# New costs for the planner, expert blocks of 224 rows, and an earlier load of the second expert's weights

## Chip, cores and metric

One core of a Trainium2 chip. The metric is device time in microseconds (us), the median of three runs. Engines as the profile names them: PE (TensorE) with its weight loads PEld, DVE (VectorE), ACT (ScalarE), POOL (GpSimd), SP (SyncE, which issues most transfers).

## The reference

Three layers in a row, on 1536 tokens of 384 values (2 batches of 768 steps, 8 heads of 48):

```python
# 1. attention: a decaying complex state for each batch and head
a = (a_re + 1j*a_im) * min(|a|, 0.999) / (|a| + 1e-6)
for t in range(768):
    S = a[t][:, None] * S + outer(k[t], v[t])
    y[t] = q[t] @ S.real
# 2. one expert of 8 for each token, capacity 384
e = argmax(x @ w_gate); g = softmax(x @ w_gate)[e]
x = g * (relu(x @ w1[e]) @ w2[e])          # w1: 384 x 1024, w2: 1024 x 384
# 3. dense layer
h = x @ w_in                                # 384 x 2048, given in float64
out = (max(h, 0) + alpha * min(h, 0)) @ w_out
```

The tokens of an expert are taken in order; those beyond its capacity of 384 give zero.

## The kernel before

**Attention.** Twelve tiles of 128 tokens. For each tile, `log_polar`, `turns` and `decay` make logarithms, phases and decays; `decay` forms exp(±sum/8) in `ar` and `ai` on ScalarE and squares each three times (`times`, L384; `DOUBLE` says on which engine, GpSimd for all of them). `edge` (L458 to L471) takes the last decay of a tile from ar. `rotate` multiplies q and k by decays (L542) and by cosine and sine (L547). `attend` transposes them (L572), evicts the transposes kT and qT on ScalarE (L577), forms scores (L591), masks them into pT on VectorE (L597), multiplies by v (L606) and by the state Z (L610), and updates Z (L649, L656). `route` picks the expert of each token and scatters its row to DRAM (`xs_d`, 384 rows for each expert) by GpSimd's indirect transfers.

The order of all this work is not the order of the code. Each operation is entered in a `Plan` with an engine, a cost (`C_ACT`, `C_TT`, `C_SQ`, ...) and a lag until its result can be used; `Plan.order` lists the operations greedily by time and rank, and that list is each engine's order of instructions. The costs act through the order alone; waits are by data. Also in the plan: `clear` zeroes `xs_d` and the unused rows of `ys_d`, and `whole` loads the first expert's weights and splits them.

**Experts.** Every product of the two feed-forward layers is made three times with float32 split into a high part (fp32r) and the rest: weights wh, wl; activations xh, xl and gh, gl. `unit(kk)` loads weight matrix kk in pieces through three staging buffers `st` (L283), rounds the high part on ScalarE (wh, L287) and subtracts on VectorE (wl, L288); matrix 2e is w1 and 2e+1 is w2 of expert e. `ffn` runs an expert's block of `SLOTS` rows in eight steps of 128 hidden units: nine products into hp (L1011) that stream SLOTS columns, gh on ScalarE (L1019) and gl on VectorE (L1020), then for each of two tiles of rows three products into y (L1001) that stream 384 columns. Hooks after each step load and split pieces of the next weights, gather the next expert's rows from `xs_d` (`gather_expert`, L1049) and store results to `ys_d` (L1209). A piece's `wh` stands on ScalarE behind the gh of its step and ahead of the next gh. All these loads wait for the last scatter:

```python
if kk < 2 * NE:
    return unit(kk, pool, eng, scatters[-1:], SYNC)
```

Before the first expert stands `overflow` (L1059): every engine reads the count of the fullest expert and branches past a slow path unless it is over SLOTS. The first expert's rows are put together on chip (`first_expert`). After the branch GpSimd scatters the gates of the first four tiles to `gs_d` (L1111).

**Dense layer.** Three chunks of 512 tokens through the same `ffn` with 16 steps and 512 columns. The first chunk's rows are gathered during the last expert from what the experts before it stored (`first_chunk_rows`, L1151 and L1162); the last expert's own are added on chip (`first_chunk_tail`).

Of the kernel before, what the change touches and what calls it, by code (L numbers as in the profile page):

```python
# [21 lines left out]
P = 128  # L22
# [4 lines left out]
NE = 8  # L27
CAP = 384
SLOTS = 256
# [38 lines left out]
class Plan:  # L68
# [9 lines left out]
    def op(self, engine, cost, fn, use=(), put=(), new=(), after=(), lag=0.06):  # L78
        n = len(self.ops)
        deps = set(after)  # L80
# [16 lines left out]
        self.ops.append(dict(engine=engine, cost=cost, fn=fn, deps=deps, new=list(new), lag=lag, rank=self.rank))  # L97
        return n

    def order(self):  # L100
# [86 lines left out]
def tile_kernel(  # L187
# [150 lines left out]
    def tensor(cost, fn, **kw):  # L338
        return plan.op("T", cost, fn, lag=0.24, **kw)
# [38 lines left out]
    def times(e, n, key):  # L378
        def fn():
            t = tl[key]  # L380
            if e == "A":
                A(out=t, in_=t, func=ACTF.Square)
            else:
                (V if e == "V" else G).tensor_tensor(out=t, in0=t, in1=t, op=ALU.mult)  # L384

        plan.op(e, {"A": C_ACT, "V": C_TT, "G": C_SQ}[e], fn, use=[key], put=[key])

    def log_polar(i):
# [14 lines left out]
        vector(C_TT, lambda: V.tensor_tensor(out=t2(), in0=t2(), in1=tl[f"ai{i}"], op=ALU.mult), use=[t, f"ai{i}"], put=[t])  # L403

        def square():
# [5 lines left out]
        plan.op(SQUARE[i], {"A": C_ACT, "V": C_TT, "G": C_SQ}[SQUARE[i]], square, use=[t], put=[w], new=[("t3", w)])  # L411
# [4 lines left out]
            use=[w, l], put=[l],  # L416
# [6 lines left out]
            use=[w, l], put=[l],  # L423
# [20 lines left out]
    def edge(i):  # L444
# [15 lines left out]
        def spread():  # L460
# [49 lines left out]
    def rotate(i):  # L510
# [13 lines left out]
        else:  # L524
            vector(
                0.4,
# [4 lines left out]
                use=[f"f{i}"], put=[c_],  # L531
# [6 lines left out]
        for dst, e, s, c in (("kk", "ai", "k", ck), ("qq", "ar", "q", cq)):  # L538
# [10 lines left out]
            vector(C_STT, scaled, use=[ek, sk], put=[ek])  # L549
            vector(C_WIDE, turned, use=[ek, c_], put=[dk], new=[(dst, dk)])  # L550

    def attend(i):
# [12 lines left out]
        def tr(hh):  # L565
            for src, nm, sc in ((kk, "kT", 1.0 / LAM), (qq, "qT", 1.0)):
# [16 lines left out]
                plan.op(e, {"A": 0.6, "V": 0.68}[e], evict, use=[p], put=[t])  # L583

        def scores(hh):
# [14 lines left out]
            vector(0.7, mask, use=[p], put=[t])  # L600
# [43 lines left out]
        scalar(0.5, out, use=[f"y{i}"], put=[f"x{i}"], new=[("x", f"x{i}")])  # L644
        if not last:
            zv = Z[:, 0:DM].rearrange("p (h d) -> p h d", d=D)
            vector(
                0.56,
# [6 lines left out]
                0.6,  # L655
# [3 lines left out]
                use=[zk, f"ez{i}"], put=[zk],  # L659
# [4 lines left out]
    def route(g):  # L664
# [11 lines left out]
        for j, i in enumerate(tl_):  # L676
# [18 lines left out]
            scalar(0.5, evict, use=[p], put=[x])  # L695
# [60 lines left out]
        vector(1.1 + 0.3 * n, choose, use=[f"lg{g}", "racc", "ready"], put=["racc", f"oc{g}"])  # L756
        tensor(0.3, count, use=[f"oc{g}", "ready"], put=[f"pp{g}"], new=[("y" if tail else "u", f"pp{g}")])
        vector(1.3, place, use=[f"pp{g}"], put=[f"si{g}"])
        for i in tl_:
# [14 lines left out]
            pool(1.2, scatter, use=[f"si{g}", f"x{i}", "zeroed"], put=[f"xs{i}"], lag=2.0)  # L774
# [5 lines left out]
    def gather_early():  # L780
        for j in range(SLOTS // P):
            rows0.append(raw.tile([P, DM], F32, tag="ar", name="rows0", bufs=RAW["ar"]))
            ins = G.dma_start(out=rows0[j], in_=xs_d[j * P:(j + 1) * P, :])
# [7 lines left out]
    def first_expert():  # L791
# [9 lines left out]
        for c in range(KC):  # L801
            for j in range(SLOTS // P):
                ins = add(c, rows0[j], ident, slice(j * P, (j + 1) * P))
# [43 lines left out]
    def clear():  # L847
# [17 lines left out]
    def whole(kk):  # L865
# [5 lines left out]
        for j in range(c // m):  # L871
# [16 lines left out]
            scalar(0.95, high, use=[key], put=[f"h{key}"])  # L888
            vector(1.05, low, use=[key, f"h{key}"], put=[f"l{key}"])
# [90 lines left out]
    def split_rows(rows, xh, xl, j, behind=None):  # L980
        pt = pm.tile([P, KC, P], F32, tag="tr", name="pt")
        for c in range(KC):
            follow(T.transpose(pt[:, c, :], rows[:, c * P:(c + 1) * P], ident), behind, "h")  # L983
        sl = slice(j * P, (j + 1) * P)
# [3 lines left out]
    def ffn(xh, xl, N, units, sink, hooks, tail=None):  # L988
        nt = N // P
        ys = [pm.tile([P, DM], F32, tag="y", name="y", bufs=4) for _ in range(nt)]  # L990
# [47 lines left out]
        for t in range(nt):  # L1038
            o = fp.tile([P, DM], F32, tag="o", name="o", bufs=3)
# [3 lines left out]
    def gather_expert(e):  # L1043
# [3 lines left out]
        for j in range(SLOTS // P):  # L1047
            rows.append(fp.tile([P, DM], F32, tag="rows", name="rows", bufs=4))
            ins = nc.sync.dma_start(out=rows[j], in_=xs_d[e * CAP + j * P:e * CAP + (j + 1) * P, :])  # L1049
# [3 lines left out]
    def split_expert(xh, xl, rows, behind):  # L1053
        for j in range(SLOTS // P):
            split_rows(rows[j], xh, xl, j, behind)
        return xh, xl

    def overflow():
        fullest = nc.values_load(most[0:1, 0:1], min_val=0, max_val=NT)  # L1059
        with tc.If(fullest > SLOTS):  # L1060
            for e in range(NE):
                r0 = e * CAP + SLOTS
                rows = fp.tile([P, DM], F32, tag="rows", name="rows", bufs=4)
                after_scatters(nc.sync.dma_start(out=rows, in_=xs_d[r0:r0 + P, :]))
# [206 lines left out]
```

## Time and profile before

| | us |
|---|---|
| median of 3 runs | 592.74 (592.65 to 595.22) |
| profiled execution | 592.36 |
| its span, first to last instruction | 590.6 |
| TensorE busy | 527.0 (89%) |
| VectorE busy | 356.2 (60%) |
| ScalarE busy | 308.5 (52%) |
| GpSimd busy | 110.7 (19%) |
| granted TensorE clock, mean | 0.949 |

Matmuls overlap, so TensorE's busy time counts a product longer than the step from one to the next; the time of a stream of products is read from the chain of waits. A group of instructions is one line of the kernel with its operation and tiles.

### The profile page before, as it was taken

The numbers are of one execution on the slowest core, as the hardware profiler recorded it, in microseconds if no ns is written. First come the engines' busy times: TensorE is split into PE (matmuls) and PEld (weight loads), VectorE is DVE, ScalarE is ACT, GpSimd is POOL, SyncE is SP. The second block draws the span as 40 slices with busy tenths as digits, with TensorE's granted clock in tenths as the row PEclk, the third lists the DMA queues.
The fourth block names the chain that finished last, engine by engine and source line by source line (L and its number), as shares of the span: only waits on it lengthen the run. The fifth ranks groups of instructions, "written<-read, shape, count | busy, mean of one in ns | idle before, by whom it ended". The sixth has DMA issues, their size and how long they took to land.

```text
span 590.6 us, 8614 instructions
## 1 busy us (share of the span) xinstructions
PE 527.0 (89%) x3270; PEld 483.3 (82%) x3270; DVE 356.2 (60%) x617; ACT 308.5 (52%) x565; POOL 110.7 (19%) x119
## 2 busy tenths in 40 slices
PE   1677969796898968799999999899999999999996
PEld 0466869795888868799999998688899999989986
DVE  2558798869638431677765796979783333333322
ACT  6577866675334231666655643446464443453433
POOL 2518084708027221000000003030200000000000
PEclk9967998899798798899999999999999999999999
DMA  8994334201000108888768746435400000010001
GB/s 281 354 344 147 95 94 139 89 14 42 0 28 1 55 29 136 275 260 257 253 205 322 234 148 222 161 130 156 149 20 35 22 0 1 0 54 2 0 2 53
DMA packets 37407, 71.01 MB, mean 120 GB/s; under 512 B 4105, under 2 KB 30098, under 8 KB 36594
## 3 DMA queue, kind: packets, MB, share of 16 engines
q1 hardware_dynamic: 35570, 65.30, 34.3%
q0 software_dynamic: 1792, 5.12, 2.5%
q8 instruction: 27, 0.44, 0.3%
q14 instruction: 18, 0.15, 0.1%
HBM read 55.84 MB, written 14.56 MB: 119 GB/s over the span
## 4 chain that ended last, share of the span: by engine, by line
PE 75%; DVE 9%; DMA 6%; POOL 3%; ACT 3%; issue 2%; SPq 0%; POOLq 0%; ACTq 0%; DVEq 0%
PE hp L1011 26%; PE y L1001 26%; PE sc L591 5%; PE y L606 4%; PE y L610 3%; DMA st<-in_moe_w 2%; PE pt L484 2%; POOL ai L384 2%; PE pkT L572 2%; DVE Z L656 2%; PE u L623 1%; POOL ar L384 1%; PE pt L487 1%; DMA gs_d<-gate,sidx 1%; PE pt L983 1%
## 5 line engine op out<-in xcount | busy, mean ns | idle before, releaser
L1011 PE MATMUL hp<-xh,wh 128*128 128x256 f32 (+1 forms) x336 | 112.5, 335 | 3.1 <-PEq L1060 2.9
L1001 PE MATMUL y<-wh,gh 128*128 128x384 f32 x320 | 109.7, 343 | 4.9 <-ACT gh L1019 4.9
L1011 PE MATMUL hp<-xl,wh 128*128 128x256 f32 (+1 forms) x336 | 111.9, 333 | 0.6 <-DVE xl L1188 0.6
L1011 PE MATMUL hp<-xh,wl 128*128 128x256 f32 (+1 forms) x336 | 111.9, 333 | 0.0
L1001 PE MATMUL y<-wl,gh 128*128 128x384 f32 x320 | 107.9, 337 | 0.0
L1001 PE MATMUL y<-wh,gl 128*128 128x384 f32 x320 | 89.3, 340 | 0.2 <-DVE gl L1020 0.2
L288 DVE TENSOR_TENSOR wl<-st,wh 128x768 fp32r<-128x768 f32 (+1 forms) x63 | 67.4, 1070 | 31.3 <-ACT wh L287 30.7
L287 ACT ACTIVATE wh<-st 128x768 fp32r<-128x768 f32 (+1 forms) x63 | 58.9, 935 | 30.6 <-DMA st<-in_moe_w 18.1
L1026 DVE SCALAR_TENSOR_TENSOR gn<-gn,nalp,gp 128x512 f32<-128x512 f32 x48 | 35.9, 748 | 62.7 <-ACT gp L1025 62.7
L1011 PEld LDWEIGHTS hp<-xh,wh 128*128 128x128 f32 x336 | 64.5, 192 | 8.6 <-issue 3.0
L1011 PEld LDWEIGHTS hp<-xl,wh 128*128 128x128 f32 x336 | 64.6, 192 | 5.7 <-DVE xl L1188 1.0
L1011 PEld LDWEIGHTS hp<-xh,wl 128*128 128x128 f32 x336 | 64.6, 192 | 5.0
L1001 PEld LDWEIGHTS y<-wh,gh 128*128 128x128 f32 x320 | 60.6, 189 | 7.4 <-ACT gh L1019 5.6
L1024 ACT ACTIVATE gn<-hp 128x512 f32<-128x512 f32 x48 | 28.7, 597 | 71.5 <-PE hp L1011 60.5
L1001 PEld LDWEIGHTS y<-wl,gh 128*128 128x128 f32 x320 | 60.5, 189 | 1.2
L1001 PEld LDWEIGHTS y<-wh,gl 128*128 128x128 f32 x320 | 56.9, 189 | 1.2 <-DVE gl L1020 0.7
L1028 DVE TENSOR_TENSOR gl<-gn,gh 128x512 fp32r<-128x512 f32 x48 | 33.1, 690 | 29.5 <-ACT gh L1027 29.4
L384 POOL TENSOR_TENSOR ar<-ar 128x384 f32<-128x384 f32 x36 | 35.2, 977 | 77.1 <-ACT ar L438 77.0
L1019 ACT ACTIVATE gh<-hp 128x256 fp32r<-128x256 f32 x64 | 24.2, 380 | 45.3 <-PE hp L1011 45.3
L606 PE MATMUL y<-vt,pT 128*128 128x128 f32 x192 | 38.8, 297 | 7.0 <-DVE pT L597 7.0
L1027 ACT ACTIVATE gh<-gn 128x512 fp32r<-128x512 f32 x48 | 30.2, 630 | 22.3 <-DVE gn L1026 21.1
L384 POOL TENSOR_TENSOR ai<-ai 128x384 f32<-128x384 f32 x36 | 40.1, 1114 | 0.0
(166 smaller groups left out, 869.3 us busy)
## 6 DMA issues: line engine op xcount, KB each, us to landing
st<-in_moe_w SPq DMA_DIRECT2D x24, 512.0 KB, 4.6
st<-in_moe_w SPq DMA_DIRECT2D x32, 384.0 KB, 3.6
sw<-in_moe_w_in SPq DMA_DIRECT2D x6, 1024.0 KB, 6.2
sw<-in_moe_w_out SPq DMA_DIRECT2D x8, 768.0 KB, 4.3
xs_d<-zero SPq DMA_DIRECT2D x1, 4608.0 KB, 15.4
ys_d<-o SPq DMA_DIRECT2D x16, 192.0 KB, 2.7
rows<-xs_d SPq DMA_DIRECT2D x14, 192.0 KB, 4.6
ar<-in_a_re SPq DMA_DIRECT2D x12, 192.0 KB, 3.8
```

Of the source, the lines that this page charges most:

```text
L287: follow(A(out=wh[:, js], in_=st, func=ACTF.Copy), behind, "A")
L288: ins = eng[j].tensor_tensor(out=wl[:, js], in0=st, in1=wh[:, js].bitcast(F32), op=ALU.subtract)
L384: (V if e == "V" else G).tensor_tensor(out=t, in0=t, in1=t, op=ALU.mult)
L591: T.matmul(out=sc[:, h, :], lhsT=tl[f"kT{i}{hh}"][:, h, :], rhs=tl[f"qT{i}{hh}"][:, h, :], start=True, stop=True)
L606: T.matmul(out=y()[:, o:o + P], lhsT=tl[f"pT{i}{hh}"][:, h, :], rhs=tl[vk][:, o:o + P], start=True, stop=(c == 0))
L1001: T.matmul(out=ys[t], lhsT=a[:, sl], rhs=b[:, f, :], start=(ft == 0 and m == 0), stop=(ft == nf - 1 and m == 2))
L1011: ins = T.matmul(out=hp, lhsT=a[:, c, fs], rhs=b[:, c, :], start=(n == 0), stop=(n == 3 * KC - 1))
L1019: last["A"] = A(out=gh, in_=hp, func=ACTF.Relu)
L1024: A(out=gn, in_=hp, func=ACTF.Relu, scale=-1.0)
L1026: V.scalar_tensor_tensor(out=gn, in0=gn, scalar=nalp[:, ft:ft + 1], in1=gp, op0=ALU.mult, op1=ALU.add)
L1027: last["A"] = A(out=gh, in_=gn, func=ACTF.Copy)
L1028: last["V"] = V.tensor_tensor(out=gl, in0=gn, in1=gh.bitcast(F32), op=ALU.subtract)
```

## The change

- `DOUBLE`: the three squarings of ar go to ScalarE, those of ai stay on GpSimd.
- All planner costs and lags are replaced by the durations from a trace. Operations get a mark `port`; marked ones of VectorE and GpSimd exclude each other in the plan. Marked are the squarings on GpSimd and VectorE's operations on two SBUF operands.
- `SLOTS` is 224 instead of 256, in two tiles of `TW` = 112 rows instead of 128. The overflow branch is taken above 224; its blocks are twice 80 rows. `clear` zeroes 160 instead of 128 rows of each expert in `ys_d`.
- The loads of weight matrix 2 (w1 of the second expert) no longer wait for the last scatter.

```diff
-SLOTS = 256
+SLOTS = 224
+ST = 2
+TW = SLOTS // ST
+OW = (CAP - SLOTS) // 2
...
-DOUBLE = (('GGG', 'GGG'),) * NTL
+DOUBLE = (('AAA', 'GGG'),) * NTL
...
-C_ACT, C_BIAS, C_TT, C_STT, C_PS, C_WIDE, C_SQ = 0.52, 0.61, 0.6, 0.62, 0.56, 1.0, 1.0
+C_ACT, C_BIAS, C_TT, C_STT, C_PS, C_WIDE, C_SQ = 0.415, 0.51, 0.47, 0.5, 0.47, 0.87, 0.79
+LAG = {'A': 0.14, 'V': 0.13, 'G': 0.1, 'T': 0.28, 'S': 2.2}
...
-    def op(self, engine, cost, fn, use=(), put=(), new=(), after=(), lag=0.06):
+    def op(self, engine, cost, fn, use=(), put=(), new=(), after=(), lag=None, port=False):
         n = len(self.ops)
+        lag = LAG[engine] if lag is None else lag
...
-                t = max([free.get(o["engine"], 0.0)] + [done[d] for d in o["deps"]])
+                t = max([free.get(o["engine"], 0.0), free.get("port", 0.0) if o["port"] else 0.0] + [done[d] for d in o["deps"]])
...
             free[o["engine"]] = t + o["cost"]
+            if o["port"]:
+                free["port"] = t + o["cost"]
...
-        plan.op(e, {"A": C_ACT, "V": C_TT, "G": C_SQ}[e], fn, use=[key], put=[key])
+        plan.op(e, {"A": C_ACT, "V": C_TT, "G": C_SQ}[e], fn, use=[key], put=[key], port=e != "A")
...
-            vector(C_STT, scaled, use=[ek, sk], put=[ek])
-            vector(C_WIDE, turned, use=[ek, c_], put=[dk], new=[(dst, dk)])
+            vector(0.53, scaled, use=[ek, sk], put=[ek], port=True)
+            vector(C_WIDE, turned, use=[ek, c_], put=[dk], new=[(dst, dk)], port=True)
...
         for e in range(NE):
-            nc.sync.dma_start(out=ys_d[e * CAP + SLOTS:(e + 1) * CAP, :], in_=zero)
-        for r in range((NE - 1) * CAP, (NE - 1) * CAP + SLOTS, P):
-            nc.sync.dma_start(out=ys_d[r:r + P, :], in_=zero)
+            nc.sync.dma_start(
+                out=ys_d[e * CAP + SLOTS:(e + 1) * CAP, :].rearrange("(r p) d -> p r d", p=OW),
+                in_=zero[0:OW].unsqueeze(1).to_broadcast([OW, 2, DM]),
+            )
+        for t in range(ST):
+            r = (NE - 1) * CAP + t * TW
+            nc.sync.dma_start(out=ys_d[r:r + TW, :], in_=zero[0:TW])
...
         if kk < 2 * NE:
-            return unit(kk, pool, eng, scatters[-1:], SYNC)
+            return unit(kk, pool, eng, scatters[-1:] if kk > 2 else (), SYNC)
...
-        for j in range(SLOTS // P):
-            rows.append(fp.tile([P, DM], F32, tag="rows", name="rows", bufs=4))
-            ins = nc.sync.dma_start(out=rows[j], in_=xs_d[e * CAP + j * P:e * CAP + (j + 1) * P, :])
+        for j in range(ST):
+            rows.append(fp.tile([TW, DM], F32, tag="rows", name="rows", bufs=4))
+            ins = nc.sync.dma_start(out=rows[j], in_=xs_d[e * CAP + j * TW:e * CAP + (j + 1) * TW, :])
...
         with tc.If(fullest > SLOTS):
-            for e in range(NE):
-                r0 = e * CAP + SLOTS
+            for e, r0 in ((e, e * CAP + SLOTS + i * OW) for e in range(NE) for i in range(2)):
...
-        ffn(*xe, SLOTS, [e], store, hooks, first_chunk_tail if e == NE - 1 else None)
+        ffn(*xe, SLOTS, TW, [e], store, hooks, first_chunk_tail if e == NE - 1 else None)
```

The rest of the diff gives new numbers and `port` marks to the other planned operations and writes tiles of TW rows where tiles of 128 stood.

## Rows read from the trace of the kernel before

**Rows 1.** Stretches: busy us (count) of PE, PEld, DVE, ACT, POOL; PEclk, DMA share, GB/s.
```profile
11.00:219.00 208.00, 171.35 (x1192) 150.85 (x1192) 141.12 (x297) 119.26 (x225) 87.36 (x87) 0.88 0.31 106
219.00:382.00 163.00, 152.72 (x1047) 148.55 (x1047) 111.52 (x169) 85.97 (x157) 10.45 (x9) 0.98 0.71 224
382.00:590.60 208.60, 202.71 (x1031) 183.65 (x1031) 100.69 (x144) 96.13 (x173) 10.76 (x8) 0.99 0.14 46
```
**Rows 2.** Waits of PE, 10 to 218 us: in total, times, longest.
```profile
PE pz L458 <- POOL ar L384: 9.0, 4, 4.6
PE y L606 <- DVE pT L597: 7.0, 3, 5.3
PE sc L591 <- ACT qT L577: 4.3, 5, 2.0
```
**Rows 3.** Stretches at the lower clock; columns as in rows 1.
```profile
114.00:120.40 6.40, 6.40 (x32) 6.33 (x33) 4.35 (x8) 3.23 (x6) 1.05 (x1) 0.50 0.10 32
149.00:155.30 6.30, 6.27 (x31) 5.80 (x31) 1.79 (x5) 1.53 (x3) 0.00 (x0) 0.56 0.00 0
186.00:194.60 8.60, 7.33 (x43) 6.55 (x42) 6.90 (x20) 2.75 (x5) 1.91 (x2) 0.66 0.01 3
...
239.90:243.30 3.40, 3.40 (x16) 3.40 (x15) 2.81 (x5) 2.40 (x5) 0.00 (x0) 0.50 0.84 275
```
**Rows 4.** One line's instructions: ns min/median/max, first and last start.
```profile
L656 DVE TENSOR_TENSOR Z<-Z,ezs x10: 548/576/7156, 47.5 to 204.5; 96x384 f32<-96x384 f32 x10
```
**Rows 5.** Timeline of POOL (start, us): first and last of nine squarings.
```profile
140.41 0.85 POOL L384 TENSOR_TENSOR ai<-ai 128x384 f32<-128x384 f32 x1
...
146.68 0.81 POOL L384 TENSOR_TENSOR ai<-ai 128x384 f32<-128x384 f32 x1
```
**Rows 6.** Chain that ended last (start, us, what), one piece each.
```profile
66.21 0.89 PE sc L591 x8
...
266.20 1.07 PE hp L1011 x9
...
465.99 2.08 PE hp L1011 x9
```
**Rows 7.** Timeline of PE in the first expert, with its idle time before.
```profile
231.04 0.44 PE L1001 MATMUL y<-wh,gh 128*128 128x384 f32 x1 [0.90 <-ACT gh L1019]
...
238.88 0.45 PE L1001 MATMUL y<-wh,gh 128*128 128x384 f32 x1 [3.03 <-ACT gh L1019]
```
**Rows 8.** Timeline of ACT in the same time.
```profile
235.89 1.06 ACT L287 ACTIVATE wh<-st 128x1024 fp32r<-128x1024 f32 x1 [4.63 <-DMA st<-in_moe_w]
```
**Rows 9.** Groups by line of POOL: busy us, mean ns, idle before.
```profile
L384 POOL TENSOR_TENSOR ai<-ai 128x384 f32<-128x384 f32 x36 | 40.1, 1114 | 0.0
L384 POOL TENSOR_TENSOR ar<-ar 128x384 f32<-128x384 f32 x36 | 35.2, 977 | 77.1 <-ACT ar L438 77.0
```
**Rows 10.** Timeline of ACT, two activations back to back.
```profile
43.43 0.93 ACT L401 ACTIVATE l<-ar 128x384 f32<-128x384 f32 x2
```
**Rows 11.** Timeline of DVE in the last expert.
```profile
368.27 0.42 DVE L1162 TENSOR_SCALAR rows<-rows,gate 128x384 f32<-128x384 f32 x1 [3.49 <-DMA rows<-ys_d,eidx]
```
**Rows 12.** The seventh expert's stretch; columns as in rows 1.
```profile
340.00:357.00 17.00, 17.00 (x126) 16.97 (x126) 16.93 (x24) 8.13 (x18) 0.00 (x0) 1.00 0.45 152
```
**Rows 13.** Transfers: count, KB each, median us from issue to landing.
```profile
xs_d<-zero SPq DMA_DIRECT2D x1, 4608.0 KB, 15.4
...
gs_d<-gate,sidx POOLq DMA_INDIRECT x4, 8.8
```
**Rows 14.** Waits of SP's queue: in total, times, longest.
```profile
SPq L283 <- DMA xs_d<-x,sidx: 2.2, 1, 2.2
```
**Rows 15.** Timeline of SP's queue (start, us of issue).
```profile
221.84 0.35 SPq L283 DMA_DIRECT2D st<-in_moe_w  x1
222.66 1.17 SPq L1049 DMA_DIRECT2D rows<-xs_d  x2
223.89 0.89 SPq L283 DMA_DIRECT2D st<-in_moe_w  x2
```

More of the change, by code (lines that the diff above doesn't have):

```diff
@@ L96, in op @@
         deps.discard(n)
-        self.ops.append(dict(engine=engine, cost=cost, fn=fn, deps=deps, new=list(new), lag=lag, rank=self.rank))
+        self.ops.append(dict(engine=engine, cost=cost, fn=fn, deps=deps, new=list(new), lag=lag, rank=self.rank, port=port))
         return n
@@ L409, in square @@
                 (V if SQUARE[i] == "V" else G).tensor_tensor(out=t3(), in0=t2(), in1=t2(), op=ALU.mult)
-        plan.op(SQUARE[i], {"A": C_ACT, "V": C_TT, "G": C_SQ}[SQUARE[i]], square, use=[t], put=[w], new=[("t3", w)])
+        plan.op(SQUARE[i], {"A": C_ACT, "V": C_TT, "G": C_SQ}[SQUARE[i]], square, use=[t], put=[w], new=[("t3", w)],
+                port=SQUARE[i] != "A")
         scalar(C_ACT, lambda: A(out=t3(), in_=t3(), func=ACTF.Ln, bias=1.0), True, use=[w], put=[w])
@@ L415, in log_polar @@
             lambda: V.scalar_tensor_tensor(out=t1(), in0=t3(), scalar=0.5, in1=t1(), op0=ALU.mult, op1=ALU.add),
-            use=[w, l], put=[l],
+            use=[w, l], put=[l], port=True,
         )
@@ L422, in log_polar @@
             lambda: V.scalar_tensor_tensor(out=t1(), in0=t1(), scalar=LN999, in1=t3(), op0=ALU.min, op1=ALU.subtract),
-            use=[w, l], put=[l],
+            use=[w, l], put=[l], port=True,
         )
@@ L530, in rotate @@
                 ),
-                use=[f"f{i}"], put=[c_],
+                use=[f"f{i}"], put=[c_], port=True,
             )
@@ L642, in out @@
             A(out=xt[i], in_=y()[:, 0:DM], func=ACTF.Copy)
-        scalar(0.5, out, use=[f"y{i}"], put=[f"x{i}"], new=[("x", f"x{i}")])
+        scalar(0.39, out, use=[f"y{i}"], put=[f"x{i}"], new=[("x", f"x{i}")])
         if not last:
@@ L658, in attend @@
                 ),
-                use=[zk, f"ez{i}"], put=[zk],
+                use=[zk, f"ez{i}"], put=[zk], port=True,
             )
@@ L772, in scatter @@
                 scatters.append(ins)
-            pool(1.2, scatter, use=[f"si{g}", f"x{i}", "zeroed"], put=[f"xs{i}"], lag=2.0)
+            pool(1.2, scatter, use=[f"si{g}", f"x{i}", "zeroed"], put=[f"xs{i}"], lag=2.0, port=False)
     early = []
@@ L978, in need, with split_rows, ffn @@
                 piece(None)
-    def split_rows(rows, xh, xl, j, behind=None):
-        pt = pm.tile([P, KC, P], F32, tag="tr", name="pt")
+    def split_rows(rows, xh, xl, j, w=P, behind=None):
+        pt = pm.tile([P, KC, w], F32, tag="tr", name="pt")
         for c in range(KC):
-            follow(T.transpose(pt[:, c, :], rows[:, c * P:(c + 1) * P], ident), behind, "h")
-        sl = slice(j * P, (j + 1) * P)
+            follow(T.transpose(pt[:, c, :], rows[0:w, c * P:(c + 1) * P], ident[0:w, 0:w]), behind, "h")
+        sl = slice(j * w, (j + 1) * w)
         A(out=xh[:, :, sl], in_=pt, func=ACTF.Copy)
         V.tensor_tensor(out=xl[:, :, sl], in0=pt, in1=xh[:, :, sl].bitcast(F32), op=ALU.subtract)
-    def ffn(xh, xl, N, units, sink, hooks, tail=None):
-        nt = N // P
-        ys = [pm.tile([P, DM], F32, tag="y", name="y", bufs=4) for _ in range(nt)]
+    def ffn(xh, xl, N, w, units, sink, hooks, tail=None):
+        nt = N // w
+        ys = [pm.tile([w, DM], F32, tag="y", name="y", bufs=4) for _ in range(nt)]
         nf = FT * len(units)
@@ L1053, in split_expert @@
     def split_expert(xh, xl, rows, behind):
-        for j in range(SLOTS // P):
-            split_rows(rows[j], xh, xl, j, behind)
+        for j in range(ST):
+            split_rows(rows[j], xh, xl, j, TW, behind)
         return xh, xl
@@ L1060, in overflow @@
         with tc.If(fullest > SLOTS):
-            for e in range(NE):
-                r0 = e * CAP + SLOTS
-                rows = fp.tile([P, DM], F32, tag="rows", name="rows", bufs=4)
-                after_scatters(nc.sync.dma_start(out=rows, in_=xs_d[r0:r0 + P, :]))
+            for e, r0 in ((e, e * CAP + SLOTS + i * OW) for e in range(NE) for i in range(2)):
+                rows = fp.tile([OW, DM], F32, tag="rows", name="rows", bufs=4)
+                after_scatters(nc.sync.dma_start(out=rows, in_=xs_d[r0:r0 + OW, :]))
                 a1 = []
@@ L1136, in first_chunk @@
             V.tensor_scalar(out=oh, in0=io, scalar1=srel[:, j:j + 1], scalar2=None, op0=ALU.is_equal)
-            for t in range(SLOTS // P):
-                T.transpose(ot[:, t, j * P:(j + 1) * P], oh[:, t * P:(t + 1) * P], identb)
+            for t in range(ST):
+                T.transpose(ot[:, t, j * P:(j + 1) * P], oh[:, t * TW:(t + 1) * TW], identb)
         os = []
-        for t in range(SLOTS // P):
-            o = fp.tile([P, n * P], F32R, tag="gn", name="os")
+        for t in range(ST):
+            o = fp.tile([TW, n * P], F32R, tag="gn", name="os")
             A(out=o, in_=ot[:, t], func=ACTF.Copy)
@@ L1172, in first_chunk_tail @@
         xh, xl, gsl, os, pts = (chunk0[k] for k in ("xh", "xl", "gsl", "os", "pts"))
-        for t in range(SLOTS // P):
-            h = fp.tile([P, DM], F32R, tag="gh", name="yh", bufs=3)
-            l = fp.tile([P, DM], F32R, tag="gl", name="yl", bufs=3)
+        for t in range(ST):
+            h = fp.tile([TW, DM], F32R, tag="gh", name="yh", bufs=3)
+            l = fp.tile([TW, DM], F32R, tag="gl", name="yl", bufs=3)
             A(out=h, in_=ys[t], func=ACTF.Copy, scale=gsl[:, t:t + 1])
```

69 lines of the change are left out of this document (35 added, 34 removed).

## The prediction

> **What bounds the kernel now.** I read the page first, then the stretch view by stage, because the share of busy time is an average over three stages with different limits [rows 1]. From 11 to 219 us (attention, routing, scatters) no engine is full: TensorE is busy 171 of 208 us at a granted clock of 0.88, VectorE 141, ScalarE 119, GpSimd 87. From 219 to 382 us (eight experts) TensorE is busy 152.7 of 163. From 382 us on (the dense layer) it is busy 202.7 of 208.6 at 0.99; nothing of the change is in that stage. So a gain must come from waits in the first stage and from TensorE work or waits in the second.
>
> The view of TensorE's waits in the first stage says what it stood for [rows 2]: 9.0 us for GpSimd's squarings of ar, 7.0 us for the masked scores pT of VectorE, 5.3 of that in one piece, and 4.3 us for ScalarE's evictions qT. Three stretches at the lower of the two clock levels (1.2 instead of 2.4 GHz) follow such gaps [rows 3].
>
> The 5.3 us piece has a visible cause. The line that multiplies Z takes 0.55 to 0.58 us, but once 7.16 us [rows 4], and in just that time GpSimd runs nine squarings back to back, from 140.41 to 147.5 us [rows 5]. VectorE, with two operands in SBUF, stood still until GpSimd's row ended.
>
> In the second stage the chain of waits is one product after another: nine first-layer products of 256 columns in 1.07 us [rows 6]. The exception is its start: TensorE waits 0.9 and 3.0 us for gh [rows 7], because ScalarE is in order and gh stands behind wh, which waits for the second expert's weights [rows 8].
>
> **Part 1, squarings and planner.** 36 squarings of ar leave GpSimd: 35.2 of its 75.3 us of squarings [rows 9]. They go to ScalarE: two activations of this size take 0.93 us, 0.465 each [rows 10], so 36 take 16.7 us. ScalarE is busy 119 of 208 us, so there is room on average; behind each squaring stand evictions like qT that TensorE waits for already. The longer half of the chain ar, ai on one engine also becomes two shorter ones: a tile's six squarings at 0.98 to 1.11 us take some 6.3 us now, then three on GpSimd, 2.3 to 3.3 us, beside three on ScalarE, 1.4.
>
> What can go at most: 9.0 us for ar and 5.3 us for the blocked Z, 14.3 together; and of the three slow-clock stretches of the stage 6.4 x 0.50 + 6.3 x 0.44 + 8.6 x 0.34 = 8.9 us. That is 23.2 us. What is late next: the other squarings, ai, which keep GpSimd and the contention (a group of two tiles still makes a row of six, 4.7 us at 0.78 each), and ScalarE. The new costs, lags and the rule that marked VectorE and GpSimd operations exclude each other only reorder each engine's queue; they cost nothing themselves, and the trace can't price an order that it hasn't seen. Bounds: nothing gained, since a new order can lose what it gains, and four fifths of 23.2, 18.6 us. I take two fifths, **-9.3 us**, since ScalarE's evictions, already the third of the waits, get 16.7 us of work in front of them.
>
> On this block the Trainium skill (SBUF — State Buffer, Who interferes with whom) says that the one of VectorE and GpSimd that starts first holds the shared port pair for its whole instruction. Read strictly, Z would have waited for one squaring; the row says nine. By the page alone the length of a GpSimd row wouldn't matter, and this term would fall by two fifths of 5.3, to -7.2 us; the measurement decides.
>
> **Part 2, blocks of 224.** The first layer streams 224 columns instead of 256. Nine products of 512 columns take 2.08 us, of 256 1.07 us [rows 6]: (2.08 - 1.07) / (9 x 256) = 0.438 ns per column, so 14.0 ns per product. 8 experts x 8 blocks x 9 products = 576, so 8.1 us. The second layer has 112 instead of 128 stationary columns but still streams 384: counted as nothing, since the chain shows products set by what they stream. The last expert can't use its 1.0 us: it waits for the rows gathered from the seventh's stores, until 368.27 us [rows 11], and that chain of transfers doesn't shorten. So **-7.1 us**. Bounds: -8.1; and -5 if the experts from 340 to 357 us gain nothing either, where VectorE is busy 16.93 of 17.00 us with weight conversions [rows 12]. Evictions, gathers and stores of 224 rows shrink by an eighth beside TensorE's work: nothing.
>
> Clearing ys_d writes 160 instead of 128 rows for each expert and 224 instead of 256 for the last: 0.34 MB more. At the 4608 KB in 15.4 us of xs_d's clearing that is 1.1 us of transfer [rows 13], with the loads of k, q, ar and ai behind it in SP's queue. No wait of TensorE for them shows after 11 us: 0, at worst +1.1.
>
> The gate of the overflow branch becomes 224. The reference's default inputs give the fullest expert 220 rows, so it stays untaken.
>
> The Trainium skill (TensorE: Matmul & The Clock Gate, Back-to-back issue gap) gives for streams of weight loads and products 81 ns at 128 columns and 131 ns at 512. As an estimate from that page 32 columns are 4.2 ns, 2.4 us in all, and the sum below would be 4.7 us higher. The trace has 229 ns at 512 and disagrees.
>
> **Part 3, the second expert's first weights.** Three loads of 512 KB (w1 of expert 1) no longer wait for the last scatter. They can't pass the branch on the fullest expert, so they start when SP leaves it: it waited 2.2 us for the scatter and issued at 221.84, the other two at 223.89, behind two gathers of rows [rows 14, 15]. Now the first goes at 219.6 and, if the gathers don't stand between, the others 0.4 us apart, before the four scatters of gates, which take 8.8 us to land and share the transfer engines [rows 13]. Before, the second wh could start only at 235.89 [rows 8]. To be won: the 3.9 us of waiting for gh, and the slow stretch at 239.9, 3.4 x 0.5 = 1.7 [rows 3]: 5.6 us. What is late next: the gathered rows, now behind 1.5 MB, and the fourth weight load, which needs a freed st buffer. Bounds 0 (the gathers keep their place in front, so only the first load moves) and 5.6; I take **-3.5 us**, nearer to the upper end because 2.2 us of head start at the front of the queue matter most while the gates' scatters haven't begun.
>
> **Sum.** -9.3 - 7.1 - 3.5 = -19.9. The profiled execution took 592.36 us (span 590.6), the median of the three runs is 592.74, so nearly the same: 592.4 - 19.9 = **572.5 us**.
>
> **Rivals.** *ScalarE takes GpSimd's place.* TensorE's waits for ScalarE grow by what those for GpSimd shrink, and part 1 gives 0: 592.4 - 10.6 = 581.8. For it: 16.7 us more on an in-order engine that feeds the scores. Against: ScalarE idles 89 of 208 us. Chance 0.22.
>
> *The early load gains nothing*, because the gathers stay in front or the gates' scatters slow it as before: 576. For it: the second load's 12 us from its issue to wh. Against: the 2.2 us wait is real. Chance 0.08.
>
> *The narrower product is slower* (the other side). No row has an fp32r product under 256 columns. If such a one ran like a plain f32 product, two records of 0.89 / 8 = 0.111 us for 128 columns each [rows 6], that is 1.74 ns per column, a product of 224 would take 0.390 instead of 0.119 us: 576 x 0.271 = +156, and 592.4 - 12.8 + 156 = 736 us. It decides against the change from 12.8 / 576 = 22 ns above the 0.119 us of now. Against: from 512 to 256 columns the time halves without a knee. Chance 0.07. The overflow branch being taken has 0.01.
>
> The forecast has the rest, 0.62, and its own range is 562 to 580. Range: it takes in both rivals on this side, 561 (four fifths of the waits, all of part 3) to 586 (nothing of part 1, 5 and about 1.5 us of the others). Below 0.5% (3 us) nothing can be told from no change. Faster 0.86 (forecast and first two rivals but for a tail of 0.06), same 0.05, slower 0.09 (the last two, and 0.01 of a bad order).
>
> **What would show it.** In the profile after: 36 activations more on ScalarE's squaring line and 36 squarings on GpSimd; no Z multiply of 7 us, and TensorE's wait for ar under 4 us; the last scatter before 212 instead of 219 us; nine products in 0.95 us; the three weight loads issued by 221 us (less the shift of the first stage) and TensorE's wait for gh under 2 us; the dense stage again 208 us. The prediction fails if nine products take over 1.07 us, if the end of the scatters doesn't move, or if TensorE's waits for ScalarE in the first stage double.

## The result

The changed kernel takes 561.07 us (median of four executions, 560.52 to 564.88) against 593.49 (592.65 to 595.22) of before: a ratio of 0.946, 95% interval 0.942 to 0.951. The forecast was 572.5 with 561 to 586: the time lies at the very edge of the range, and the sum behind it came out so only because two errors partly cancel. The profiled execution took 561.13 us, span 559.0.

The stretch view of after, cut at the first product of the first expert and the first 512-column product of the dense layer (columns as in [rows 1]):

```profile
0.00:186.90 186.90, 157.31 (x1193) 138.50 (x1193) 124.89 (x306) 139.06 (x273) 54.62 (x69) 0.95 0.42 137
186.90:348.70 161.80, 148.83 (x1046) 144.10 (x1046) 105.44 (x166) 83.57 (x155) 6.87 (x7) 0.96 0.75 215
348.70:559.00 210.30, 203.79 (x1032) 183.49 (x1032) 101.47 (x146) 96.62 (x174) 11.23 (x8) 0.99 0.15 49
```

The same cuts through before stand at 221.7 and 381.4 us:

```profile
0.00:221.70 221.70, 171.63 (x1193) 151.16 (x1193) 144.72 (x306) 126.86 (x237) 91.54 (x105) 0.88 0.34 114
221.70:381.40 159.70, 152.22 (x1047) 148.34 (x1047) 110.23 (x167) 84.92 (x155) 8.45 (x7) 0.98 0.72 225
381.40:590.60 209.20, 203.19 (x1032) 183.81 (x1032) 101.29 (x145) 96.73 (x174) 10.76 (x8) 0.99 0.14 47
```

So the first stage became 34.8 us shorter (forecast 9.3), the experts 2.1 us longer (forecast 10.6 shorter: 7.1 and 3.5), the dense layer 1.1 us longer (forecast 0).

In the first stage TensorE does the same 1193 products in 157.3 instead of 171.6 us, at a granted clock of 0.95 instead of 0.88, and idles 29.6 instead of 50.1 us. Its waits in after, 10 to 184 us (in total, times, longest):

```profile
PE pl L445 <- DVE l L431: 10.1, 1, 10.1
PE pz L467 <- ACT ar L389: 5.6, 2, 4.0
PE pz L467 <- DMA k<-in_k: 4.4, 1, 4.4
PE y L615 <- DVE pT L606: 2.2, 4, 0.7
PE sc L600 <- ACT qT L586: 0.9, 1, 0.9
```

The first row is the start-up. Not only the wait for ar is smaller [rows 2]: pT fell from 7.0 to 2.2 us, qT from 4.3 to 0.9. The Z multiply that once took 7.16 us [rows 4] takes at most 1.16 us (one line's instructions, ns min/median/max):

```profile
L665 DVE TENSOR_TENSOR Z<-Z,ezs x10: 542/548/1161, 41.8 to 168.7; 96x384 f32<-96x384 f32 x10
```

In the experts nine products of 224 columns take 0.99 to 1.00 us in the chain of waits, where 256 took 1.07 [rows 6]:

```profile
226.60 0.99 PE hp L1024 x9
...
236.43 1.00 PE hp L1024 x9
```

And the second expert's weights come no sooner. The timeline of SP's queue:

```profile
187.43 0.69 SPq L290 DMA_DIRECT2D st<-in_moe_w  x1
190.98 0.48 SPq L1062 DMA_DIRECT2D rows<-xs_d  x2
191.51 0.90 SPq L290 DMA_DIRECT2D st<-in_moe_w  x2
```

GpSimd's timeline, the last scatter of rows and the first of four of gates:

```profile
183.87 1.01 POOL L770 DMA_INDIRECT xs_d<-x,sidx  x1 [0.30 <-issue]
185.18 0.97 POOL L1123 DMA_INDIRECT gs_d<-gate,sidx  x1 [0.30 <-issue]
```

ScalarE's timeline, the first two pieces of w1 of the second expert:

```profile
195.52 1.06 ACT L294 ACTIVATE wh<-st 128x1024 fp32r<-128x1024 f32 x1 [6.02 <-DMA gs_d<-gate,sidx]
203.68 1.06 ACT L294 ACTIVATE wh<-st 128x1024 fp32r<-128x1024 f32 x1 [6.86 <-DMA st<-in_moe_w]
```

The order is that of before [rows 15]: one load, two gathers, two loads. The second load needs 12.2 us from its issue at 191.51 to wh at 203.68; before it was 12.0 (223.89 to 235.89, [rows 8, 15]). TensorE waits for gh 2.9 and 4.6 us instead of 0.9 and 3.0 [rows 7] (its waits, 184 to 220 us: in total, times, longest):

```profile
PE y L1014 <- ACT gh L1032: 7.5, 2, 4.6
```

The first expert takes 31.5 us instead of 27.3, the second 22.2 instead of 20.4, so the two lose 6.0 us. The first expert's stretch, in after and in before, columns as in [rows 1]:

```profile
186.90:218.36 31.46, 22.78 (x127) 21.49 (x127) 11.14 (x17) 10.99 (x20) 2.48 (x3) 0.77 0.86 177
```

```profile
221.70:248.95 27.25, 22.35 (x131) 21.21 (x132) 11.84 (x18) 11.29 (x20) 2.90 (x3) 0.87 0.82 201
```

It also runs at a lower granted clock, 0.77 instead of 0.87: in the 2 us ahead of it the clock is 0.50 in after and 1.00 in before.

### The profile page after: what moved, and what is told of

Same layout as the page of the kernel before. It is cut to its first block, busy times and chain, and to the rows that moved or that the text cites. A ratio compares the mean times of both kernels' runs of the same rounds, so it can differ in the third digit from the quotient of the medians.

```text
span 559.0 us, 8603 instructions
## 1 busy us (share of the span) xinstructions
PE 509.9 (91%) x3270; PEld 466.1 (83%) x3270; DVE 331.8 (59%) x617; ACT 319.3 (57%) x601; POOL 72.7 (13%) x83
## 4 chain that ended last, share of the span: by engine, by line
PE 45%; DMA 10%; issue 5%; DVE 3%; ACT 2%; POOL 1%; SPq 0%; POOLq 0%; ACTq 0%
PE y L1014 23%; PE hp L1024 22%; DMA st<-in_moe_w 5%; DMA rows<-ys_d,gidx 2%; DMA ys_d<-o 1%; DVE wl L295 1%; DMA rows<-ys_d,eidx 1%; ACT wh L294 1%; PE pt L996 1%; DVE st L283 0%; POOL rows L1110 0%; ACT o L1053 0%; DMA out<-o 0%; POOL rows L1163 0%; DVE gl L1033 0%
## 5 line engine op out<-in xcount | busy, mean ns | idle before, releaser
L1014 PE MATMUL y<-wh,gh 128*128 128x384 f32 (+1 forms) x320 | 109.2, 341 | 7.6 <-ACT gh L1032 7.5
L1024 PE MATMUL hp<-xh,wh 128*128 128x224 f32 (+1 forms) x336 | 111.1, 331 | 3.3 <-DVEq L1073 2.1
L1024 PE MATMUL hp<-xl,wh 128*128 128x224 f32 (+1 forms) x336 | 110.8, 330 | 1.8 <-DVE xl L999 1.0
L1024 PE MATMUL hp<-xh,wl 128*128 128x224 f32 (+1 forms) x336 | 110.7, 329 | 0.0
L1014 PE MATMUL y<-wl,gh 128*128 128x384 f32 (+1 forms) x320 | 108.1, 338 | 0.0
L1014 PE MATMUL y<-wh,gl 128*128 128x384 f32 (+1 forms) x320 | 89.5, 341 | 1.3 <-DVE gl L1033 1.0
L1014 PEld LDWEIGHTS y<-wh,gh 128*128 128x128 f32 (+1 forms) x320 | 58.7, 183 | 10.0 <-ACT gh L1032 7.9
L1014 PEld LDWEIGHTS y<-wl,gh 128*128 128x128 f32 (+1 forms) x320 | 58.7, 183 | 1.5
L1014 PEld LDWEIGHTS y<-wh,gl 128*128 128x128 f32 (+1 forms) x320 | 55.2, 184 | 3.2 <-DVE gl L1033 2.2
L615 PEld LDWEIGHTS y<-vt,pT 128*128 128x128 f32 x192 | 29.3, 198 | 3.5 <-DVE pT L606 3.0
```

Of the source, the lines that this page charges most:

```text
L615: T.matmul(out=y()[:, o:o + P], lhsT=tl[f"pT{i}{hh}"][:, h, :], rhs=tl[vk][:, o:o + P], start=True, stop=(c == 0))
L1014: T.matmul(out=ys[t], lhsT=a[:, sl], rhs=b[:, f, :], start=(ft == 0 and m == 0), stop=(ft == nf - 1 and m == 2))
L1024: ins = T.matmul(out=hp, lhsT=a[:, c, fs], rhs=b[:, c, :], start=(n == 0), stop=(n == 3 * KC - 1))
```

## The experiments

Twelve kernels ran. Stage times are those of each one's profile: first stage (to the first expert's first product), experts, dense layer. Ratios are to the kernel before, run beside it.

| kernel | median us | ratio, 95% interval | first stage | experts | dense |
|---|---|---|---|---|---|
| before | 593.49 | | 221.7 | 159.7 | 209.2 |
| after | 561.07 | 0.946 (0.942 to 0.951) | 186.9 | 161.8 | 210.3 |
| e1, squarings alone | 582.88 | 0.985 (0.982 to 0.989) | 211.2 | 159.2 | 209.2 |
| e2, costs and lags alone | 585.83 | 0.991 (0.987 to 0.994) | 214.4 | 160.0 | 209.0 |
| e3, costs, lags, port marks | 582.13 | 0.980 (0.972 to 0.988) | 207.9 | 166.2 | 210.5 |
| e4, costs, lags, squarings | 565.01 | 0.957 (0.951 to 0.962) | 191.8 | 158.7 | 209.2 |
| e12, lags and squarings | 572.40 | 0.966 (0.960 to 0.972) | 202.2 | 159.0 | 209.2 |
| e5, after with 256 rows | 561.90 | 0.948 (0.942 to 0.954) | 186.2 | 164.7 | 209.5 |
| e6, after with the wait back | 556.48 | 0.936 (0.932 to 0.941) | 187.6 | 159.4 | 209.9 |
| e7, gates moved in the code | 560.53 | 0.944 (0.939 to 0.948) | 186.6 | 161.6 | 209.9 |
| e8, loads ahead of gathers | 560.23 | 0.943 (0.936 to 0.951) | 184.8 | 159.9 | 212.0 |
| e9, gates held back | 559.92 | 0.946 (0.942 to 0.951) | 186.4 | 161.7 | 209.3 |
| e10, loads before the branch | 552.53 | 0.935 (0.930 to 0.940) | 186.6 | 152.7 | 210.2 |
| e11, e9 and e10 | 554.37 | 0.937 (0.933 to 0.941) | 188.0 | 154.0 | 210.2 |

Each stage time is of one execution. After and e5 to e11 have the same plan for the first stage, and its time in their eight profiles goes from 184.8 to 188.0 us, so a difference of two or three microseconds between two such times shows nothing.

### The first stage: e1 to e4 and e12

**e1**, before with one edit:

```diff
-DOUBLE = (('GGG', 'GGG'),) * NTL
+DOUBLE = (('AAA', 'GGG'),) * NTL
```

> Before with one edit: the three squarings of ar of each group go to ScalarE (DOUBLE 'AAA','GGG'), with the old costs, the old lags and no port marks. The first stage (to the first product of the first expert) took 221.7 us before and 186.9 after, 34.8 less. Theory A (the squarings on GpSimd and what they block on VectorE held the stage): at least 22 of the 34.8 come back, first expert's product by 200 us, whole time 572 or less. Theory B (the order made from the new costs and lags did it): under 12 us, first product after 210, time 581 or more. Theory C (the port marks did it): likewise under 12 us; B and C part in the next runs.

Measured: 211.2, that is 10.5 us less. Theory A falls, as B and C wanted: the squarings alone bring a third of the 34.8, about what the forecast had for the whole part. GpSimd's squarings already stand in rows of three here, and no VectorE instruction of the stage takes over 1.27 us: the blocked Z multiply is gone, and 24.3 us of the gain are still to come from elsewhere.

**e2**, before with the new `C_...` costs and `LAG`, but `DOUBLE` old and no port in `Plan.order`.

> Before with the new costs and lags of the planner alone; all squarings stay on GpSimd and no operation excludes another. Theory A: the 36 GpSimd squarings of ar still stand in front of TensorE, gain under 8 us, first product after 213, time 585 to 593. Theory B: at least 18 us, first product by 204, time 575 or less. Theory C: under 8 us, as A.

Measured: 7.3 us less, so theory B falls as well, as put. The longest VectorE instruction, in its timeline:

```profile
133.95 7.09 DVE L428 SCALAR_TENSOR_TENSOR l<-l,w 128x384 f32<-128x384 f32 x1 [1.24 <-ACT w L425]
```

GpSimd's timeline, the first and the last of eight:

```profile
134.31 0.86 POOL L388 TENSOR_TENSOR ar<-ar 128x384 f32<-128x384 f32 x1
...
139.81 0.82 POOL L388 TENSOR_TENSOR ai<-ai 128x384 f32<-128x384 f32 x1
```

The block of [rows 4, 5] has only moved to another line: eight squarings in a row on GpSimd, and VectorE stands from just ahead of their start until just after their end. New costs don't remove it.

**e3**, the same with the port marks.

> The run before with the port marks added: the planner counts a VectorE operation on SBUF operands and a GpSimd squaring as excluding each other; squarings still all on GpSimd. Theory A: within 5 us of the run before. Theory B: the same. Theory C: at least 12 us less than the run before, and no Z multiply of 7 us.

Measured: the median is 3.7 us under that of e2, and the intervals overlap. Its profiled execution was the longest of its four (586.37), so the 207.9 us of its first stage, 6.5 less than e2, is no firm figure, and its expert stage is not read. Theory C wanted 12 us and no blocked Z multiply. One of 4.3 us is still there, and another instruction takes 5.6 (VectorE's timeline):

```profile
125.59 5.64 DVE L407 TENSOR_TENSOR t<-t,ai 128x384 f32<-128x384 f32 x1
```

beside six squarings on GpSimd (first and last in its timeline):

```profile
126.07 0.84 POOL L388 TENSOR_TENSOR ar<-ar 128x384 f32<-128x384 f32 x1
...
130.00 0.82 POOL L388 TENSOR_TENSOR ai<-ai 128x384 f32<-128x384 f32 x1
```

The marks shape the planner's order; each engine then goes through its queue as its data come, and the two rows above show that this can bring a blocked instruction all the same.

**e4**, costs, lags and `DOUBLE`, no port marks.

> New costs and lags and the squarings of ar on ScalarE, but no port marks; blocks of 256 and the old loads. Theory A and B: the full 34.8 us of the first stage, first product at 185 to 190, time 556 to 562 since the expert stage is that of before. Theory C: 10 us or more are lacking, first product after 197.

Measured: 191.8, that is 29.9 us less. No VectorE instruction takes over 1.84 us. So the two edits that bring 10.5 and 7.3 us alone bring 29.9 together: 12.1 us belong to neither. The port marks give the other 5 us (191.8 to 186.9; e5, with 256 rows as e4, has 186.2), less than theory C's 10; the first product comes just behind the 185 to 190 of A and B. In GpSimd's timeline e4 has its squarings in threes but for one row of six and one of three that is split; after has twelve rows of three, the longest 4.9 us, where before had rows of up to twelve.

**e12**, squarings and lags with the old costs:

```diff
-    def op(self, engine, cost, fn, use=(), put=(), new=(), after=(), lag=0.06):
+    def op(self, engine, cost, fn, use=(), put=(), new=(), after=(), lag=None):
...
+        lag = LAG[engine] if lag is None else lag
```

> Before with the squarings of ar on ScalarE and the new lags alone, no new cost, no port marks. Squarings alone gave 211.2 us to the first expert's first product, squarings with costs and lags 191.8. Theory M (the old plan hands results over too early, 0.06 us against 0.13 and 0.14, and so orders consumers in front of work that is ready): at least 12 of the 19.4 come from the lags, first product by 199, time 570 or less. Rival N (the old costs overstate the operations by a fifth, so that the engines' shares in the plan are wrong): under 6 us from the lags, first product after 205, time 577 or more.

Measured: 202.2, between M and N. One row of five squarings is left, and beside it a Z multiply of 3.2 us (its line's instructions, then the row in GpSimd's timeline):

```profile
L658 DVE TENSOR_TENSOR Z<-Z,ezs x10: 543/548/3157, 46.8 to 184.3; 96x384 f32<-96x384 f32 x10
```

```profile
160.27 4.30 POOL L386 TENSOR_TENSOR ai<-ai 128x384 f32<-128x384 f32 x5
```

On top of the squarings the lags bring 9.0 us and the costs 10.4. Neither theory of one culprit holds. TensorE's idle and busy time in the first stage, from the stretch views:

| | first stage | idle | busy | clock |
|---|---|---|---|---|
| before | 221.7 | 50.1 | 171.6 | 0.88 |
| squarings | 211.2 | 41.2 | 170.0 | 0.90 |
| squarings, lags | 202.2 | 40.8 | 161.4 | 0.93 |
| squarings, lags, costs | 191.8 | 32.8 | 159.0 | 0.95 |
| after | 186.9 | 29.6 | 157.3 | 0.95 |

In this order, squarings and costs remove idle time (8.9 and 8.0 us), the lags shorten the same products (8.6 us) at a higher clock. The length of the rows doesn't set this: e12, with a blocked multiply of 3.2 us, is 9.0 us ahead of e1, which has none. Which instructions the new order moved to win it was not followed. Of the 34.8 us, 20.5 are idle time and 14.3 busy time. From 60 to 160 us of after next to nothing more is to be had from waits: TensorE is busy 98.1 of 100 us at full clock.

```profile
60.00:110.00 50.00, 49.00 (x396) 43.42 (x394) 44.85 (x96) 49.15 (x99) 17.40 (x15) 1.00 0.39 117
110.00:160.00 50.00, 49.11 (x427) 45.30 (x427) 39.05 (x97) 35.72 (x72) 15.91 (x17) 1.00 0.06 23
```

### The blocks of 224: e5

```diff
-SLOTS = 224
+SLOTS = 256
```

> After with blocks of 256 rows again (two tiles of 128), all else as after. Theory D (224 columns save what the row of nine products says, 0.07 us per nine, 64 blocks, 4.6 us, and nothing else changes): slower than after by 3.5 to 6 us, nine products 1.07 us. Rival E (the new tile of 112 rows costs at its evictions, transposes or transfers what the columns save; that is why the expert stage grew by 2.2 us): the same as after within 1.5 us or faster, and expert 1 to 6 in under 17 us each.

Measured: 561.90, the same as after within intervals that are too wide to tell theory D's 3.5 us from nothing. The fifth to seventh expert from store to store, in e5's terms 17.52, 17.71 and 16.94 us, are in after 16.97, 17.07 and 17.06. (The third and fourth, 17.7 and 17.6, are 16.6 and 16.0, but with fewer instructions between their stores, so they are not read so finely.) The sixth and seventh of after:

```profile
290.08:307.15 17.07, 17.07 (x130) 16.97 (x129) 11.61 (x18) 11.04 (x21) 0.00 (x0) 1.00 0.79 247
307.15:324.21 17.06, 17.06 (x130) 17.01 (x128) 16.09 (x24) 8.74 (x19) 0.00 (x0) 1.00 0.54 166
```

An expert that TensorE's products set gains about 0.6 us, which is eight times the 0.07 of nine products. The seventh gains nothing: VectorE is busy 16.1 of its 17.1 us [rows 12]. The eighth waits for its gathered rows. The first two wait for weights (below): 53.7 us in after against 51.2 in e5, which takes back most of what the four in the middle gain. In these two profiles the expert stage of after is still 2.9 us shorter (161.8 against 164.7), and the first stage and the dense layer are 0.7 and 0.8 us longer. So theory D's mechanism holds in the middle of the stage; E's doesn't, since the experts of 256 rows there take 17.5 to 17.7 us, not under 17. Which of the two has the whole time right stays open.

### The early load and the gates: e6 to e11

**e6**, after with the old wait:

```diff
-            return unit(kk, pool, eng, scatters[-1:] if kk > 2 else (), SYNC)
+            return unit(kk, pool, eng, scatters[-1:], SYNC)
```

> After with the second expert's first weights waiting for the last scatter again. Theory F (the early load gains nothing, since the gathers and the gates' scatters stand where they stood): within 1.5 us of after, wh of the first expert's stage at the same distance from the last scatter. Rival G (the forecast, -3.5 us): slower than after by 2.5 to 5 us.

Measured: 556.48, 4.6 us faster than after; against e7, whose GpSimd queue is that of after and which ran beside it, 4.0 us (the intervals overlap from 0.939 to 0.941). Both views fall: by these medians the edit doesn't gain nothing or 3.5 us, it costs. Every engine issues the same instructions in the same order in both kernels; only the wait for the last scatter moves from the first load to the gathers behind it. The load leaves at 187.85 us, no sooner than in after, the gathers 0.8 us behind it instead of 3.6, and the second wh starts 13.5 us after the first product instead of 16.8. SP's queue in e6:

```profile
187.85 0.35 SPq L290 DMA_DIRECT2D st<-in_moe_w  x1
188.69 3.18 SPq L1062 DMA_DIRECT2D rows<-xs_d  x2
191.93 1.11 SPq L290 DMA_DIRECT2D st<-in_moe_w  x2
```

ScalarE's timeline, the second piece:

```profile
201.08 1.06 ACT L294 ACTIVATE wh<-st 128x1024 fp32r<-128x1024 f32 x1 [3.55 <-DMA st<-in_moe_w]
```

That 512 KB ahead of the last scattered rows hold them up fits this, but no run isolates it. The wait explains only part of what the first two experts lose: they take 51.3 us in e6, 53.7 in after, and 46.8 to 47.9 in before, e1, e2, e4 and e12, which have 256 rows and the old wait. What costs e6 the other 3.4 us or more was not isolated.

**e7**, after with the gates' scatters written into the fifth expert:

```diff
-            if e == 0:
+            if e == 4:
                 scatter_gates()
```

> After with the four scatters of the gates issued in the fifth expert instead of the first; they are needed only in the last one. Theory H (the four scatters of 128 elements of 4 bytes hold the transfer engines, so that the weights of the second expert come at 30 to 100 GB/s for 12 us): the second st load takes under 6 us instead of 12.1, TensorE's waits for gh in the first expert fall from 7.5 us to under 3, the first expert takes 26 us or less instead of 31.5, and the whole is 3 to 7 us faster than after. Rival I (the loads are slow because four queues of gathers and weights share the engines, or the first expert is slow through its half clock alone): under 1.5 us, and the fifth expert may lose what the first gains.

Measured: 560.53, as after, and it says nothing of H: with no dependency to hold them, the scatters kept their old place in GpSimd's queue, ahead of the branch (184.90 us).

**e8**, the three loads of w1 of expert 1 issued by `preload` (shown under e10) right behind the branch, ahead of the first expert's hooks.

> After with the three loads of the second expert's first weights issued together right behind the branch, ahead of the two gathers of rows; the conversions stay where they were. Theory J (what held the second and third load was the gathers' wait for the scatters in front of them): all three issued by 189 us instead of 191.5 and 194, the wait of TensorE for gh down from 7.5 to under 5 us, 1 to 3 us faster than after. Rival H (the gates' scatters slow any load that is under way from 185 to 198): the loads land no earlier than before, within 1 us of after.

Measured: 560.23, within 1 us of after. The loads were issued from 184.76 us on without a gap and TensorE's waits for gh fell from 7.5 to 2.6 us, so J's mechanism is there; the experts take 1.9 us less, the dense layer 1.8 us more in this profile.

**e9**, the gates' scatters held by a wait:

```diff
+            tc.add_manual_dep(ins.ins, behind.ins.name, SYNC, reason="not before the fifth expert")
```

> After with the four scatters of the gates held behind a product of the fifth expert by a wait; in the earlier attempt (e7) GpSimd issued them where it always had, ahead of the branch, so it moved nothing. Theory H (the scatters of 4-byte elements hold the transfer engines while the second expert's weights load): in the 12 us after the first expert's first product the rate is over 150 GB/s throughout instead of 23 to 35 in parts, the second st load takes under 7 us instead of 12, the first two experts take 49 us or less instead of 53.7, and the whole is 3 to 6 us faster than after. Rival I (the gathers of rows from the tensor just scattered, or code loading, are what is slow): the slow stretch stays, under 1.5 us gained.

Measured: H's mechanism holds, its price doesn't. With the same order on SP, the second load's wh comes 4.4 us after its issue instead of 12.2 (188.83 to 193.25) and no wait for gh is left in the first expert, which takes 22.0 instead of 31.5 us. The rate in the first 14 us of the first expert, after (three stretches) and e9 (three):

```profile
186.90:190.90 4.00, 4.00 (x19) 4.00 (x20) 0.39 (x1) 0.36 (x1) 2.48 (x3) 0.50 0.77 23
190.90:192.90 2.00, 2.00 (x16) 2.00 (x16) 0.00 (x0) 0.00 (x0) 0.00 (x0) 0.93 0.77 298
192.90:200.90 8.00, 4.51 (x23) 3.85 (x21) 1.52 (x2) 1.30 (x2) 0.00 (x0) 0.82 0.98 53
```

```profile
186.40:190.40 4.00, 3.97 (x19) 4.00 (x19) 0.39 (x1) 0.49 (x2) 0.00 (x0) 0.50 0.69 197
190.40:192.40 2.00, 2.00 (x13) 2.00 (x13) 1.04 (x1) 1.17 (x2) 0.00 (x0) 0.73 1.08 320
192.40:200.40 8.00, 7.92 (x59) 7.72 (x58) 4.52 (x8) 4.52 (x8) 0.00 (x0) 1.00 0.80 235
```

The transfer engines are as busy either way (last but one column), but with the gates under way they move 23 and 53 GB/s. In the fifth expert the scatters do the same again. It takes 23.4 us instead of 17.0, and the second, at a granted clock of 0.86 instead of 1.00, 24.5 instead of 22.2: 8.7 of the 9.5 us are given back there. The first of the four in GpSimd's timeline:

```profile
265.49 0.97 POOL L1123 DMA_INDIRECT gs_d<-gate,sidx  x1 [81.14 <-PE hp L1024]
```

Two stretches of 2 us behind them, columns as before:

```profile
270.00:272.00 2.00, 2.00 (x15) 1.99 (x14) 0.97 (x2) 0.30 (x1) 0.29 (x1) 1.00 1.47 80
272.00:274.00 2.00, 2.00 (x20) 2.00 (x18) 0.39 (x1) 0.06 (x1) 0.00 (x0) 1.00 0.42 25
```

**e10**, the loads issued ahead of `overflow`, whose slow path gets its weight buffer from another pool:

```diff
+    def preload(kk=2):
+        for j in range(KC):
+            pre[kk, j] = stp.tile([P, 1, FE], F32, tag="st", name=f"st{kk}", bufs=3)
+            preins[kk, j] = nc.sync.dma_start(
...
+    preload()
     overflow()
...
-                    a1.append(stp.tile([P, FE], F32, tag="st", name="a1", bufs=3))
+                aw = wB.tile([P, KC, FE], F32, tag="wh", name="a1")
```

> After with the three loads of the second expert's first weights issued ahead of the branch on the fullest expert, so that they can land while the last tiles are routed (the overflow branch gets its buffers from another pool). Theory K (in after the loads can't leave before SP passes the branch, so they gained nothing; ahead of it they do): the three wh conversions start by 190 us instead of 195 to 206, TensorE's waits for gh in the first expert are under 2.5 us instead of 7.5, the first two experts take 47 to 50 us instead of 53.7, the whole is 4 to 7 us faster than after. Rival L (the gathered rows and the half clock hold the first expert anyway, and the next loads wait instead): under 1.5 us.

Measured: 552.53, 8.5 us faster than after, with separate intervals; theory K. The loads leave at 103.5 and 110.3 us, as soon as the staging buffers are free, and the three conversions wait for nothing. SP's queue:

```profile
103.50 1.46 SPq L257 DMA_DIRECT2D st<-in_moe_w  x2
...
110.32 0.33 SPq L257 DMA_DIRECT2D st<-in_moe_w  x1
```

ScalarE's timeline, the last of the three:

```profile
192.41 1.05 ACT L304 ACTIVATE wh<-st 128x1024 fp32r<-128x1024 f32 x1
```

TensorE waits 1.7 us for gh; the first expert takes 23.9 us, the second 23.3. The gates' slow stretch is still there, but no load is due in it. The eighth expert, at 19.9 instead of 22.7 us, gives another 2.8, since its gathered rows land sooner; why was not tried.

**e11**, e9 and e10 together.

> The loads ahead of the branch and the gates held behind the fifth expert. If H and K both hold: faster than either, by 1 to 3 us against the better one, 551 to 555. If only one holds: the same as that one within 1.5 us.

Measured: 554.37, no better than e10. The first two experts fall to 20.0 and 20.5 us, and the fifth pays 23.2 instead of 17.0.

## Why the prediction came out as it did

**Part 1 was mis-sized and its bound was wrong.** The forecast counted the squarings at -9.3 us and the planner's new numbers at nothing ("they cost nothing themselves"). Squarings alone measured -10.5. The step that failed is the other: lags and costs add 19.4 us on top, the port marks 5. The bound of -18.6 was worked out from two waits and three slow stretches with a visible cause, 23.2 us. [Rows 1] had more: TensorE idle for 36.7 of 208 us, and a granted clock of 0.88, which between the levels 0.50 and 1.00 is some 50 us at the lower one (an estimate: 208 x 0.12 x 2), where the three stretches listed are 21.3. With a better order pT, qT and other short waits shrank too, and the same products took 14.3 us less where 8.9 were listed.

**The blocked Z multiply was read rightly, but a long row doesn't always block.** Blocks of 7.09, 5.64 and 3.2 us stay beside rows of eight, six and five squarings (e2, e3, e12); in after, with rows of three, no VectorE instruction of the stage takes over 1.22 us. Before also had longer rows that let VectorE in between: beside one of twelve the same Z multiply took 1.18 us (VectorE's timeline, then the first and the last of the twelve in GpSimd's):

```profile
47.50 1.18 DVE L656 TENSOR_TENSOR Z<-Z,ezs 96x384 f32<-96x384 f32 x1
```

```profile
46.34 0.83 POOL L384 TENSOR_TENSOR ar<-ar 128x384 f32<-128x384 f32 x1 [15.03 <-ACT ar L438]
...
57.49 0.93 POOL L384 TENSOR_TENSOR ai<-ai 128x384 f32<-128x384 f32 x1
```

The Trainium skill (SBUF — State Buffer, Who interferes with whom) has the wait end with one instruction of the other engine. The row of twelve agrees with that (1.18 us), the 7.16, 7.09 and 5.64 us don't: there the wait ended with the row. What decides between the two was not found.

**ScalarE did not take GpSimd's place**: 36 squarings cost it 18.9 us (0.525 each, forecast 0.465). TensorE's waits for ScalarE between the start-up and the scatters fell from 11.3 to 8.6 us, though 5.6 of these are now for ar, more than the "under 4 us" that the prediction named as a sign.

**Part 2 was mis-sized twice.** A product became 8 to 9 ns shorter (0.07 to 0.08 us in nine), not 14.0: the columns from 512 to 256 don't extrapolate to 224. That is 576 x 8.3 = 4.8 us at most. And only the experts that products set keep it, some 0.6 us each in the middle of the stage: the seventh is VectorE's, as the lower bound had it (with the last and the seventh left out the sum is 6.1, not the 5 written there), and the first two, which the sum counted in full, wait for weights. The estimate worked out from the Trainium skill (TensorE: Matmul & The Clock Gate, Back-to-back issue gap), 2.4 us in all, was too low for the products as the row was too high.

**Part 3 failed as its rival said.** The step that failed is the overlap: the gathers kept their place and the gates' scatters slowed the loads, so the wait for gh grew from the 3.9 us that the prediction counted to 7.5 where it was to go; by e6 moving the wait made the kernel some 4 us slower. Behind the branch no load could start sooner, which the forecast knew (2.2 us of head start) and still priced at 3.5. Ahead of the branch (e10) the same loads are worth 8.5 us beyond after.

The dense layer takes 0.6 to 1.1 us over before's 209.2 in most kernels with 224 rows (e9 0.1, e8 2.8); this was not followed up.

**The rest of the sum.** 34.8 us gained where 9.3 were forecast, and 3.2 lost where 10.6 were to be gained: the error of one part (25.5) hid that of the others (13.8). That the total came within the range is luck as much as reading: the squarings alone were sized about right, the two other parts were not.

## What to carry over

Here a planner's costs and lags were worth more than the work that was moved between engines: bound such an edit by all of the waiting engine's idle and slow-clock time, not by waits with a visible culprit. Two such edits can be worth more together than apart (29.9 us against 10.5 and 7.3). Ask of an early transfer from where on its queue can issue it; here a branch ahead of it counted for more than the wait that was taken away. A gain in one stage's products is had only in the blocks that those products set.

## What was not expected of the hardware

Four indirect scatters of 128 elements of 4 bytes each brought the transfer rate to 23 and 53 GB/s for 12 us of the first expert (197 and 235 with the scatters elsewhere) and, moved to the fifth expert, to 80 and 25 GB/s for 4 us, and that expert took 6.4 us longer. In after, transfers are less dense in the seventh expert (0.54 busy); scatters put there were not tried.
